# New ranks for the first and last steps of a hand-ordered two-layer kernel, and a small load on another queue

## The chip, the cores and the metric

The kernel runs on one core of a Trainium2 chip. The metric is the device time of one execution in microseconds, the median of three runs. One more execution was recorded by the hardware profiler, and all rows shown here are from it.

## The reference

Two layers, A and B, are applied twice in turn to a sequence x of 2048 rows of 640 numbers, each on the normalized sequence and with a residual:

```python
x = x + _A_ref(_layernorm(x), A_mem0, A_Wq, A_Wk, A_Wv, A_Wo, A_seg_len)
x = x + _B_ref(_layernorm(x), B_w1, B_w2, B_w3, B_w4)
x = x + _A_ref(_layernorm(x), ...)      # the same weights again
x = x + _B_ref(_layernorm(x), ...)
```

A is attention with a recurrent memory. The sequence is cut into 64 segments of 32 rows. For each segment, 8 memory rows and the 32 segment rows (40 together) go through attention with 32 heads of 192, under a causal mask that leaves the memory visible. The first 8 rows of the result are the memory of the next segment, so the segments of one layer must be done one after the other:

```python
for s in range(n_seg):
    h = concatenate([mem, x[:, s * 32:(s + 1) * 32]], axis=1)
    q, k, v = (einsum('btd,dhe->bhte', h, W) for W in (Wq, Wk, Wv))
    scores = where(mask, einsum('bhqe,bhke->bhqk', q, k) * scale, -1e9)
    o = einsum('bhte,hed->btd', einsum('bhqk,bhke->bhqe', softmax(scores), v), Wo)
    mem = o[:, :8]
    outs.append(o[:, 8:])
```

B is a mixer with an MLP: layernorm, w1 (640 x 640), GELU, four column groups shifted by one or two rows forward or back, w2 (640 x 640), a residual, layernorm, w3 (640 x 1536), GELU, w4, a residual. All data are bf16.

## The kernel before

**Lanes and steps.** The first A layer is lane 0 and the second one lane 1, five segments behind it. A step t of 69 does segment t of lane 0 and segment t - 5 of lane 1 together: 80 columns of activations per matmul where both lanes are there, which is so in steps 5 to 63. Steps 0 to 4 and 64 to 68 have one lane only (40 columns, computed 56 wide). Every second step, a chunk of 64 rows of each lane runs through B (functions `chunk` and `chunk_end`) beside the attention; chunk 0 begins in step 2, and the last chunk runs alone after step 68.

**A step.** `attention_step` goes over the 32 heads in 8 groups of 4, two groups to a pair of weight columns. For a group: keys and queries (L1638, tiles psk and psq, 30 matmuls each), the copies of them by VectorE and ScalarE, values (L1743 with one lane, tile psv, 10 matmuls of 384 columns for each half pair), scores (L1763, pss, 6 matmuls), the softmax on VectorE and ScalarE, a transpose (L1798, pst, 4), the product with the values (L1815, pso, 8), and the output projection (L1841, psy, two halves of 15). The single buffers for keys, queries and probabilities tie a group to the one before it.

**Weights.** Part of the attention weights stays in SBUF (`res_tile`, loads at L1480), the rest is streamed again in every step through a ring of 12 slots (`load_pair`, L1496); the last pair of a step is kept for the next. The weights of B go through a ring of 3 slots (`load_b`, L1532 to L1538). All of these are issued by SyncE (SP), whose list is in order: a load that waits holds those behind it. Step 0 loads all attention weights once, 31.5 MB.

**The order.** Every operation is entered with `add` in a `Plan`. Each engine has one list, sorted by the operation's `pr`, which is the start of its step (48 to a step) plus a number from the table `RANK`, found by the part's tag, the function's name and how often it came. The tags of the two-lane steps 7 to 61 are `step0` and `step1`, those of their chunks `chunk` and `chunk_end`; the steps at the two ends have tags of their own (`first`, `second`, `head2` to `head6`, `tail0` to `tail5`, `end`, `last`, `last_end`, and `chunk_0` and the like). Equal ranks are taken in the order in which they were entered:

```python
lines = {e: sorted((o for o in self.ops if o.e == e), key=lambda o: (o.pr, o.i)) for e in engines}
```

`place` then walks through the lists with a model of durations. It gives out PSUM and ring slots and says which SP loads are held back until a certain matmul is done. It never changes the order within an engine.

**The ends.** `start` loads the 8 memory rows (L2385) into `vx2`, a part of the buffer h2u that VectorE clears first, and the first 128 input rows (L2400), both on SP. At the end of a chunk, `ft4` (L2371, tile psn) transposes its normalized rows for lane 1; ScalarE copies them to where the attention reads them. In the last chunk the twelve row blocks of w4 (L2324, tile y) are taken in four parts of three, each after its GELU and for each of two column halves.

Of the kernel before, what the change touches and what calls it, by code (L numbers as in the profile page):

```python
# [8 lines left out]
ACT = mybir.ActivationFunctionType  # L9
# [64 lines left out]
        "apply_ln.f": (5823623, 14711714, 41344890, 50140480,),  # L74
        "chunk.f1": (-282353,),
        "chunk.f2": (-279353,),
        "chunk.f3": (11931231,),
        "chunk.fe": (11885669,),
        "chunk.fe3": (51644685,),
        "chunk.fel": (11888669,),  # L80
        "chunk.fhr": (29147201,),
        "chunk.fhs": (48728121,),
        "chunk.fk0": (-242386,),
        "chunk.fk1": (29099225,),
        "chunk.fs": (50134480, 50137480,),
        "chunk.ft": (276821,),
        "chunk.ftl": (16247520,),
        "chunk.fw": (27423019, 27290948, 27355567, 45544174, 42382384, 42537930, 53199095, 51647685, 52014009,
            61485311, 60294121, 61862243, 68553475,),
        "chunk.fx": (463310,),  # L90
        "chunk.fx0": (19284882, 15974063,),
        "chunk.fxu": (52262814,),
# [6 lines left out]
        "load_b.fn": (-11648251, -10043186, -10061451, 28210158, 27695754, 26335880, 37821417, 39249861,  # L99
            39863368, 52700349, 52565225, 55051271, 61800496,),  # L100
        "transposes.f": (7724019, 50355195,),
    },
    "chunk_0": {
        "apply_ln.f": (4538124, 5597588, 28417407,),
        "chunk.f1": (-57885499,),
        "chunk.f2": (-52174124,),
        "chunk.f3": (5635096,),
        "chunk.fe": (5984368,),
        "chunk.fe3": (30624721,),
        "chunk.fel": (7390477,),  # L110
        "chunk.fhr": (12978596,),
        "chunk.fhs": (21983325,),
        "chunk.fk0": (3941774,),
        "chunk.fs": (26770777, 26773777,),
        "chunk.ft": (287279,),
        "chunk.ftl": (8154259,),
        "chunk.fw": (10898172, 11428325, 9816535, 22114487, 22111506, 22106575, 35230677, 31585055, 36089115,
            42297789, 43852725, 42859895, 51136238,),
        "chunk.fx": (26689,),
        "chunk.fx0": (9696294, 8940053,),  # L120
        "chunk.fxu": (31869412,),
# [6 lines left out]
        "load_b.fn": (-50643732, -54844896, -50893189, 13355857, 10512466, 13802419, 26207666, 25044572,  # L128
            30162184, 34930868, 36974992, 36093962, 41994092,),
        "transposes.f": (5241977, 28420407,),  # L130
    },
    "chunk_1": {
        "apply_ln.f": (5188177, 5304240, 16754321, 34290954,),
        "chunk.f1": (-3885035,),
        "chunk.f2": (2878183,),
        "chunk.f3": (11030708,),
        "chunk.fe": (10677253,),
        "chunk.fe3": (35559227,),
        "chunk.fel": (14015378,),
        "chunk.fhr": (16787571,),  # L140
        "chunk.fhs": (27232205,),
        "chunk.fk0": (-2386666,),
        "chunk.fk1": (8785106,),
        "chunk.fs": (30730498, 30733498,),
        "chunk.ft": (-66578,),
        "chunk.ftl": (11033708,),
        "chunk.fw": (15374235, 15374235, 15374235, 28977346, 29252606, 27401998, 36668792, 35592102, 36728839,
            44065631, 47134963, 44719301, 50340601,),
        "chunk.fx": (480073,),
        "chunk.fx0": (12535502, 11391513,),  # L150
        "chunk.fxu": (34730386,),
# [6 lines left out]
        "load_b.fn": (-12025702, -12014120, -11721377, 20176838, 21353444, 15499060, 30530966, 28177755,  # L158
            30530966, 36977269, 38686929, 38033259, 44520182,),
        "transposes.f": (8162117, 34343668,),  # L160
    },
    "chunk_2": {
        "apply_ln.f": (4731456, 6523101, 17796726, 29088164,),
        "chunk.f1": (-17894593,),
        "chunk.f2": (2893951,),
        "chunk.f3": (6655158,),
        "chunk.fe": (7220521,),
        "chunk.fe3": (32398753,),
        "chunk.fel": (11058085,),
        "chunk.fhr": (15897759,),  # L170
        "chunk.fhs": (28856856,),
        "chunk.fk0": (2451823,),
        "chunk.fk1": (11780324,),
        "chunk.fs": (26979944, 26982944,),
        "chunk.ft": (1151586,),
        "chunk.ftl": (7727683,),
        "chunk.fw": (13670250, 13670706, 13746357, 22235702, 22955237, 26645082, 34320431, 34254360, 33960831,
            45657603, 44775551, 43775707, 61169734,),
        "chunk.fx": (273607,),
        "chunk.fx0": (10743432, 11542267,),  # L180
        "chunk.fxu": (29054564,),
# [6 lines left out]
        "load_b.fn": (-17872484, -14843409, -32827582, 17069457, 17605094, 17567464, 26421363, 26389164,  # L188
            23014726, 36743531, 42403460, 34896909, 44579461,),
        "transposes.f": (5188954, 31624248,),  # L190
    },
    "chunk_end": {
        "apply_ln.f": (92798701,),
        "chunk_end.fc": (92804701, 103908174, 95145945,),
        "chunk_end.fs": (87395771, 87477590,),
        "chunk_end.fst": (88627127, 94644354,),
        "chunk_end.ft4": (92801701,),
        "chunk_end.fw": (75064939, 84266408, 74209536, 76906110, 85870768, 84840446,),
        "chunk_loads.f": (89254710, 94354887, 91668152, 91838190, 91163514,),
        "ln_ops.f1": (88627127,),  # L200
        "ln_ops.f2": (90742589,),
        "load_b.fn": (70817954, 75700858, 60623461, 70394650, 76123229, 75884221,),
    },
    "chunk_end_0": {
        "apply_ln.f": (96080479,),
        "chunk_end.fc": (104851242, 103783179,),
        "chunk_end.fs": (86548528, 87483179,),
        "chunk_end.fst": (89850784,),
        "chunk_end.ft4": (96083479,),
        "chunk_end.fw": (62060627, 62060627, 71462733, 77227245, 76430775, 83316611,),  # L210
        "chunk_loads.f": (88185073, 89080724, 85358214,),
        "ln_ops.f1": (90380445,),
        "ln_ops.f2": (91641311,),
        "load_b.fn": (42877559, 42623100, 62941044, 70087169, 68888715, 77038207,),
    },
    "chunk_end_1": {
        "apply_ln.f": (70510275,),
# [1047 lines left out]
def kernel(  # L1265
# [1117 lines left out]
    def start():  # L2383
        def f1(op):
            nc.sync.dma_start(out=vx2[0:M, :], in_=A_mem0[0])  # L2385
# [96 lines left out]
```

## Time and profile before

| | us |
|---|---|
| median of 3 runs | 3204.87 (3199.76 to 3208.84) |
| the profiled execution | 3210.39 |
| its span, first to last instruction | 3208.7 |
| TensorE busy | 3092.8 (96%) |
| VectorE, ScalarE, GpSimd busy | 2049.6, 1712.3, 504.2 |
| TensorE busy from 300 to 600 us | 294.27 of 300 |
| TensorE busy from 0 to 300 us | 235.75 of 300 |
| TensorE busy from 2860 to the end | 318.38 of 349 |

PE is TensorE's matmul unit, PEld its weight loads, which run beside the matmuls; DVE is VectorE, ACT ScalarE, POOL GpSimd and SP SyncE. A row of the view of waits reads: who waited, at which line, for what; then the total in us, how often, and the longest. "issue" stands for idle time in which the engine waited for nothing that the profile shows. A row of the view of windows reads: from and to in us, the length, the busy us of each engine with the number of its instructions, the share of TensorE's full clock that was granted, the busy share of the DMA engines, and GB/s. A row of the timeline reads: start, length, engine, line, operation, tiles, count, and in brackets the idle time before it and what ended that. A row of the chain reads: start, length, what, count.

### The profile page before, as it was taken

To read this page: it belongs to the slowest core of one execution; us is meant where nothing else is said; L and a number is where in the kernel's file an instruction comes from. 1 tells how busy PE (TensorE), PEld (TensorE's weight loads), DVE (VectorE), ACT (ScalarE), POOL (GpSimd) and SP (SyncE) were. 2 spreads that over 40 slices of the span, in tenths; PEclk is the share of its full clock that TensorE was granted. 3 is DMA by queue.
4 is the path that set the end of the run, shared out by engine and by line. 5 is a ranking of instruction groups with operands and counts; after the bars stand their busy time and mean duration, and the time that the engine had idled before them with its cause. 6 is when DMAs were issued, how large, how long until landed. Compare 5 with 4: busy or idle time off the path is not lost.

```text
span 3208.7 us, 158772 instructions
## 1 busy us (share of the span) xinstructions
PE 3092.8 (96%) x70198; PEld 2761.7 (86%) x70201; DVE 2049.6 (64%) x6448; ACT 1712.3 (53%) x3985; POOL 504.2 (16%) x983
## 2 busy tenths in 40 slices
PE   4889999999999999999999999999999999999997
PEld 3778888888888988988889889888998888888886
DVE  2556666666666666666666666666666666666565
ACT  1334555555556555555565556555555565555443
POOL 0001111111111111111111111111111111110000
PEclk8999999999999999999999999999999999999999
DMA  9777888888888887888888888877887788888786
GB/s 362 263 258 263 262 271 258 260 264 281 260 262 283 271 259 261 266 282 259 260 284 267 256 263 267 279 258 259 282 271 256 258 279 267 261 267 282 243 291 219
DMA packets 421674, 859.45 MB, mean 268 GB/s; under 512 B 48334, under 2 KB 216223, under 8 KB 420984
## 3 DMA queue, kind: packets, MB, share of 16 engines
q1 hardware_dynamic: 396792, 796.09, 75.7%
q0 software_dynamic: 24032, 53.12, 5.2%
q8 instruction: 550, 9.01, 1.1%
q14 instruction: 140, 1.15, 0.1%
q10 hardware_dynamic: 160, 0.08, 0.0%
HBM read 823.73 MB, written 25.37 MB: 265 GB/s over the span
## 4 chain that ended last, share of the span: by engine, by line
PE 89%; DMA 5%; issue 3%; DVE 1%; ACT 1%; POOL 0%; SPq 0%; POOLq 0%; ACTq 0%; DVEq 0%
PE psq L1638 17%; PE psk L1638 17%; PE psy L1841 17%; PE psv L1685 12%; PE pso L1815 4%; PE pss L1763 4%; PE y L2317 3%; PE psh L2271 3%; PE psv L1712 3%; PE pst L1798 2%; PE psv L1743 2%; DMA V<-vahead 2%; DMA wst<-in_A_Wq_dram 2%; PE hs L2208 1%; PE psh L2148 1%
## 5 line engine op out<-in xcount | busy, mean ns | idle before, releaser
L1638 PEld LDWEIGHTS <-wst 128*128 128x128 bf16 x19872 | 830.4, 99 | 92.5 <-issue 22.3
L1841 PE MATMUL psy<-oT,wo 128*128 128x80 bf16 (+1 forms) x16560 | 679.1, 200 | 14.0 <-issue 10.0
L1673 ACT CAST V<-psv 32x384 bf16<-32x384 f32 (+3 forms) x1032 | 479.1, 473 | 376.2 <-PE psv L1685 159.8
L1841 PEld LDWEIGHTS <-wo 128*128 128x128 bf16 x16560 | 619.1, 99 | 29.0 <-issue 27.2
L1638 PE MATMUL psk<-hT,wst 128*128 128x80 bf16 (+1 forms) x9936 | 562.1, 200 | 25.6 <-DMA wst<-in_A_Wk_dram 13.0
L1638 PE MATMUL psq<-hT,wst 128*128 128x80 bf16 (+1 forms) x9936 | 540.8, 200 | 13.3 <-DMA wst<-in_A_Wq_dram 10.9
L1648 ACT CAST qT<-psq 128x480 bf16<-128x480 f32 (+1 forms) x552 | 293.8, 532 | 393.6 <-PE psq L1638 353.7
L1775 DVE CUSTOM_DVE_ANT_1 pss<-pss,mask 80x320 f32<-80x320 f32 (+2 forms) x552 | 258.8, 469 | 319.8 <-PE pss L1763 298.3
L1663 DVE CAST kT<-psk 64x160 bf16<-64x160 f32 (+1 forms) x1104 | 338.9, 307 | 84.1 <-PE psk L1638 60.5
L1823 ACT CAST oT<-pso 128x480 bf16<-128x480 f32 (+1 forms) x552 | 293.5, 532 | 161.9 <-PE pso L1815 147.2
L1782 ACT ACTIVATE Pm<-pss,sm 80x320 bf16<-80x320 f32 (+2 forms) x552 | 279.1, 506 | 165.7 <-PE pst L1798 83.1
L1786 DVE TENSOR_REDUCE sm<-Pm 80x4 f32<-80x320 bf16 (+2 forms) x552 | 251.1, 455 | 122.4 <-ACT Pm L1782 113.7
L1638 PE MATMUL psq<-hT,wq 128*128 128x80 bf16 (+1 forms) x6624 | 316.2, 200 | 8.7 <-DMA wq<-in_A_Wq_dram 5.3
L1806 ACT COPY PT<-pst 80x320 bf16<-80x320 bf16 (+2 forms) x552 | 220.7, 400 | 188.3 <-PE pso L1815 105.7
L1638 PE MATMUL psk<-hT,wk 128*128 128x80 bf16 (+1 forms) x6624 | 315.8, 200 | 2.0 <-issue 1.1
L1685 PEld LDWEIGHTS <-hT 128*128 128x128 bf16 x2320 | 206.7, 98 | 104.9 <-issue 1.0
L1656 DVE CAST kT<-psk 128x320 bf16<-128x320 f32 (+1 forms) x552 | 253.3, 459 | 55.6 <-PE psk L1638 46.5
L1638 PEld LDWEIGHTS <-wq 128*128 128x128 bf16 x6624 | 266.5, 99 | 21.9 <-issue 12.8
L1685 PE MATMUL psv<-wv,hT 128*128 128x384 bf16 x1276 | 284.1, 326 | 0.5 <-ACT V L1673 0.5
L1788 DVE TENSOR_TENSOR Pm<-Pm,sm 80x320 bf16<-80x320 bf16 (+2 forms) x552 | 255.7, 463 | 44.7 <-DVE sm L1787 1.0
L1638 PEld LDWEIGHTS <-wk 128*128 128x128 bf16 x6624 | 266.7, 99 | 3.1 <-issue 2.5
L1693 POOL DMA_DIRECT2D vahead<-V x232 | 119.5, 516 | 953.6 <-ACT V L1673 727.7
(136 smaller groups left out, 4126.4 us busy)
## 6 DMA issues: line engine op xcount, KB each, us to landing
wst<-in_A_Wk_dram SPq DMA_DIRECT2D x556, 384.0 KB, 4.7
wst<-in_A_Wq_dram SPq DMA_DIRECT2D x556, 384.0 KB, 4.8
wstB<-in_B_w_dram SPq DMA_DIRECT2D x495, 320.0 KB, 4.5
wst<-in_A_Wv_dram SPq DMA_DIRECT2D x383, 384.0 KB, 5.0
wstB<-in_B_w_dram SPq DMA_DIRECT2D x132, 160.0 KB, 4.1
vahead<-V POOLq DMA_DIRECT2D x232, 84.0 KB, 4.3
V<-vahead POOLq DMA_DIRECT2D x232, 84.0 KB, 4.7
wo<-in_A_Wo_dram SPq DMA_DIRECT2D x8, 960.0 KB, 12.3
```

What stands on the lines that cost most here:

```text
L1638: nc.tensor.matmul(out=o[:, cc, 0:W], lhsT=wv(kc, GW * j + cc * P, GW * j + (cc + 1) * P), rhs=h[:, kc, cw:cw + W], start=begin(pq), stop= ...
L1648: nc.scalar.copy(out=qT[G % QT_BUFS][:, :, c0:c0 + N], in_=T(pq)[:, :, off:off + N])
L1656: nc.vector.tensor_copy(out=k4[:, :, 0::3, c0:c0 + N], in_=p4[:, :, 0::2, off:off + N])
L1663: copy(out=k4[r0:r1, :, jj, c0:c0 + N], in_=p4[r0:r1, :, 1, off:off + N])
L1673: (nc.vector.tensor_copy if e == "DVE" else nc.scalar.copy)(out=v_part(*dst), in_=a_)
L1685: nc.tensor.matmul(out=T(bank)[:], lhsT=left[:, kc, :], rhs=wv(kc, GWH * b, GWH * (b + 1)), start=(kc == 0), stop=(kc == KC - 1))
L1775: nc.vector.tensor_tensor_reduce(out=o, in0=o, in1=maskt.unsqueeze(1).to_broadcast([NR, HG, N]), scale=-scale, scalar=3.0e38, op0=ALU.add, ...
L1782: nc.scalar.activation(out=Pb[0:NR, :, 0:N], in_=o, func=ACT.Exp, bias=sm_[0:NR, 0:1], scale=-1.0)
L1786: nc.vector.tensor_reduce(out=sm_[0:NR, 2:2 + HG], in_=Pb[0:NR, :, 0:N], axis=AX.X, op=ALU.add)
L1788: nc.vector.tensor_tensor(out=Pb[0:NR, :, 0:N], in0=Pb[0:NR, :, 0:N], in1=sm_[0:NR, 6:6 + HG].unsqueeze(2).to_broadcast([NR, HG, N]), op=A ...
L1823: nc.scalar.copy(out=o_[:, :, off:off + N], in_=T(pso)[:, :, 0:N])
L1841: nc.tensor.matmul(out=o[:, m, cw:cw + W], lhsT=wo[:, cc, m * P:(m + 1) * P], rhs=o_[:, cc, 0:W], start=st, stop=True, skip_group_check=True)
```

## The change

The table `RANK` is replaced as a whole. Its numbers are in units of 1/67108864 (2 to the 26th) where they were millionths, and `add` is changed to match. For `step0`, `step1`, `chunk` and `chunk_end` the numbers are the old ones on the new scale. For all other tags they are from a new search: the order of the one-lane steps 0 to 4 and 64 to 68, of the two-lane steps next to them, of the chunks beside these, and of the last chunk. The search's plan counted TensorE's instruction blocks; the kernel's own plan does not. Apart from that, the load of the memory rows goes to ScalarE's queue. No operation is added or left out.

```diff
     "chunk": {
-        "chunk.f3": (11931231,),
+        "chunk.f3": (800691382,),
...
     "chunk_end_tail0": {
-        "apply_ln.f": (81876355,),
-        "chunk_end.fst": (82366936, 81760822,),
-        "chunk_end.ft4": (83228689,),
-        "ln_ops.f2": (81873355,),
+        "apply_ln.f": (5872788644,),
+        "chunk_end.fst": (5628179420, 5628240926,),
+        "chunk_end.ft4": (5992579053,),
+        "ln_ops.f2": (5628142308,),
...
     "last_end": {
-        "chunk_end.fs": (27670453, 24358356,),
-        "chunk_end.fw": (21564715, 21306200, 23454463, 22051901, 27667453, 23690061, 23690061, 23690061,),
+        "chunk_end.fs": (3903370521, 3903370521,),
+        "chunk_end.fw": (3165677059, 3058847649, 3701121311, 3165878386, 3903169194, 3903169194, 3902455248,
+            3900429352,),
...
     "start": {
-        "start.f1": (-606783133,),
-        "start.f4": (-606786133,),
+        "start.f1": (-761774171496,),
+        "start.f4": (-762032755413,),
...
-        op.pr = round(1000000 * due) if k >= len(ranks) else round(1000000 * self.base) + ranks[k]
+        op.pr = round(67108864 * due) if k >= len(ranks) else round(67108864 * self.base) + ranks[k]
...
     def start():
         def f1(op):
-            nc.sync.dma_start(out=vx2[0:M, :], in_=A_mem0[0])
-        add("SP", 0.1, -90, f1, w=(B("vx2"),), dma=20000)
+            nc.scalar.dma_start(out=vx2[0:M, :], in_=A_mem0[0])
+        add("ACT", 0.1, -90, f1, w=(B("vx2"),), dma=20000)
```

Some pieces of the two orders, read from the sorted ranks:

| | before | after |
|---|---|---|
| SP's first entries | input rows, memory rows, load, load, resident tile | input rows, load, load, load, resident tile |
| last Q or K tile of step 0, MB into its loads | 26.7 | 26.0 |
| last V tile of step 0 | 27.5 | 29.5 |
| last loads of step 0 | two Wo tiles | two Wo tiles |
| matmuls between the last w4 matmul and psn, chunks tail0, tail1, tail2 | 147, 102, 72 | 282, 102, 102 |
| last w4 work of the last chunk (part of four, column half) | 3rd second half, 4th both halves, 3rd first half | 4th both halves, 3rd both halves |

More of the change, by code (lines that the diff above doesn't have):

```diff
@@ L87 @@
[L87 to L92, printed above, removed]
[6 rows of a table removed]
[L99 to L101 removed]
+        "apply_ln.f": (390816740, 987286415, 2774608591, 3364870645,),
@@ L107 @@
[L107 to L118, printed above, removed]
@@ L131 @@
+        "chunk.fx0": (367754743, 172569584,),
+        "chunk.fxu": (1938774438,),
[6 rows of a table added]
+        "load_b.fn": (-170906047654, -170906047654, -170906047654, 920004857, 882220319, 896865883,
+            1304411523, 1257239965, 1386097304, 2462708421, 2481349681, 2470811516, 2484920200,),
+        "transposes.f": (164006783, 1639917844,),
     },
     "chunk_1": {
[L133 to L136, printed above, removed]
@@ new lines @@
+        "chunk.fe": (316376284,),
+        "chunk.fe3": (1959638099,),
+        "chunk.fel": (369464748,),
+        "chunk.fhr": (778257113,),
+        "chunk.fhs": (1679713241,),
+        "chunk.fk0": (646066165,),
+        "chunk.fk1": (898552330,),
+        "chunk.fs": (1715148724, 1715350050,),
+        "chunk.ft": (57711930,),
+        "chunk.ftl": (169733834,),
+        "chunk.fw": (807022150, 806116800, 807023775, 1271841077, 1402935676, 1121619675, 2204982466,
+            1956421294, 1956443760, 2937607038, 3058004067, 2968056114, 3969956053,),
@@ L301 @@
-        "transposes.f": (6585971, 28518353,),
+        "apply_ln.f": (97288509, 505476737, 1074913445, 1893060360,),
+        "chunk.fe": (327833962,),
+        "chunk.fe3": (2026986560,),
+        "chunk.fel": (534071399,),
+        "chunk.fhr": (859836856,),
+        "chunk.fhs": (1844791763,),
+        "chunk.fk0": (266312925,),
+        "chunk.fk1": (787177492,),
+        "chunk.fs": (1674764092, 1863774978,),
+        "chunk.ft": (-23764831,),
+        "chunk.fw": (638420884, 661797947, 628306519, 1566545467, 1562896270, 1559653263, 2046135994,
+            2027187887, 2124823259, 2620748490, 2816149302, 2636649469, 3162075176,),
@@ L327 @@
-        "transposes.f": (6527484, 35837665,),
+        "apply_ln.f": (371605162, 370993904, 1393728099, 2093210348,),
+        "chunk.fe": (460332473,),
+        "chunk.fe3": (2296318838,),
+        "chunk.fel": (609297303,),
+        "chunk.fhr": (796384097,),
+        "chunk.fhs": (2296117511,),
+        "chunk.fk0": (693286516,),
+        "chunk.fk1": (693487842,),
+        "chunk.fs": (1747505621, 1942032597,),
+        "chunk.ft": (12500783,),
+        "chunk.fw": (679901984, 611651605, 752911618, 1704347815, 1714078083, 1736058533, 2660864586,
+            2596069770, 2714677185, 2972142262, 2984054357, 2984033548, 3917670881,),
@@ L351 @@
-        "load_b.fn": (-7573298, -3992147, -5434168, 18870690, 18402542, 15297474, 27659785, 24913866,
-            27115241, 35610124, 33976492, 35065580, 44270645,),
-        "transposes.f": (11703929, 31113333,),
+        "apply_ln.f": (812472994, 901319518, 1463224163, 1911689701,),
+        "chunk.fe": (875636097,),
+        "chunk.fe3": (2230136542,),
+        "chunk.fel": (875837424,),
+        "chunk.fhr": (1136613167,),
+        "chunk.fhs": (1876018868,),
+        "chunk.fk0": (574183471,),
@@ new lines @@
+        "chunk.fx": (-278567231,),
+        "chunk.fxu": (1297854132,),
+        "chunk.fz0": (-6543789675,),
+        "chunk.halves.fa": (-216070822, -216292776, 282927822, 1297416848,),
+        "chunk.halves.fn": (-216292776, -216292776,),
+        "gelu.f1": (-215890123, 248054344, 1298055458, 1304618073, 1384067416, 1320313861,),
+        "gelu.f2": (-216292776, 252139152, 1298256785, 1304416746, 1431936661, 1362814397,),
+        "gelu.f3": (252340479, 252340479, 1305020726, 1350736613, 3339755119, 1414490168,),
```

1565 lines of the change are left out of this document (803 added, 762 removed), and 300 rows, old and new, of the table RANK.

## The prediction

> **What bounds the kernel now.** I read the page's summary first, then the busy shares by slice, then the chain.
>
> ```profile
> span 3208.7 us, 158772 instructions
> PE 3092.8 (96%) x70198; PEld 2761.7 (86%) x70201; DVE 2049.6 (64%) x6448; ACT 1712.3 (53%) x3985; POOL 504.2 (16%) x983
> PE   4889999999999999999999999999999999999997
> q8 instruction: 550, 9.01, 1.1%
> PE 89%; DMA 5%; issue 3%; DVE 1%; ACT 1%; POOL 0%; SPq 0%; POOLq 0%; ACTq 0%; DVEq 0%
> ```
>
> TensorE is busy 96% of the span and carries 89% of the chain. It is short of nine tenths only in the first three slices and the last, and those, with the one-lane steps in them, are all that this change reorders. I therefore sorted the ranks of the diff (they are the sort keys of each engine's list, so the diff gives the order outright). For the 55 two-lane steps 7 to 61 and their chunks the new ranks are the old ones times 67.108864, the ratio of the two scales, and the order is the same on SP, ACT, DVE and (one instruction at the edge apart) POOL. On TensorE the two halves of one output projection, 15 matmuls each on the same operands, swap in the even steps: nothing. So every gain or loss must come from the first 300 us and the last 290 us.
>
> The fourth row is the key to those parts. 550 packets of 9.01 MB make 16.4 KB each, and TensorE's 70198 matmuls and 70201 weight loads over 550 give 255 instructions a packet: TensorE's code arrives in blocks of about 128 matmul pairs. The next view counts matmuls (the x behind PE busy) between starts that the trace marks as idle "issue", that is, waiting for nothing it can see.
>
> ```profile
> 106.60:125.61 19.01, 17.68 (x512) 14.90 (x511) 11.01 (x44) 8.42 (x26) 0.00 (x0) 1.00 0.90 307
> ...
> 165.54:186.65 21.11, 17.73 (x510) 15.39 (x511) 11.79 (x45) 8.48 (x26) 0.00 (x0) 0.99 0.75 238
> 186.65:209.94 23.29, 21.30 (x512) 17.52 (x511) 11.25 (x43) 8.45 (x25) 0.79 (x2) 0.93 0.92 309
> 209.94:236.00 26.06, 22.47 (x639) 19.44 (x639) 17.99 (x68) 9.98 (x32) 4.73 (x9) 0.93 0.66 222
> ```
>
> 512, 510, 512 and 639 are four, four, four and five times 128. The unexplained stalls sit on the block boundaries. What they cost in the one-lane steps, at the head (95 to 262 us) and then at the tail (2960 to 3181 us):
>
> ```profile
> PE psy L1841 <- issue: 5.1, 5, 1.5
> PE pso L1815 <- issue: 3.2, 2, 1.8
> PE psq L1638 <- issue: 2.2, 2, 1.8
> ...
> PE psk L1638 <- issue: 0.4, 1, 0.4
> ```
>
> ```profile
> PE psn L2371 <- DVE h2u L1911: 2.4, 2, 1.8
> PE psy L1841 <- issue: 1.7, 3, 1.2
> PE psq L1638 <- DMA wst<-in_A_Wq_dram: 1.6, 2, 1.4
> PE psv L1743 <- issue: 1.4, 2, 0.9
> ...
> PE psh L2271 <- issue: 1.0, 1, 1.0
> PE pst L1798 <- issue: 1.0, 1, 1.0
> ```
>
> Head: 5.1 + 3.2 + 2.2 + 0.4 = 10.9 us. Tail: 1.7 + 1.4 + 1.0 + 1.0 = 5.1 us. Together 16.0 us, and no other wait in these parts comes near that.
>
> The first step is another matter:
>
> ```profile
> 5.00:10.00 5.00, 1.93 (x27) 1.56 (x28) 1.01 (x4) 0.58 (x3) 2.98 (x6) 1.00 0.86 285
> 10.00:50.00 40.00, 12.35 (x282) 11.48 (x279) 4.15 (x19) 1.93 (x6) 0.00 (x0) 0.79 1.03 393
> 50.00:87.50 37.50, 28.09 (x549) 20.67 (x547) 13.62 (x50) 9.98 (x30) 1.16 (x3) 0.77 1.05 381
> 87.50:94.30 6.80, 4.55 (x105) 4.06 (x106) 2.43 (x11) 2.05 (x6) 0.49 (x1) 0.75 0.63 173
> ```
>
> The last two columns are the share of the DMA engines and GB/s. From about 6 to 87.5 us they are full at 381 to 393 GB/s. The four attention weights are 4 x 640 x 6144 x 2 bytes = 31.5 MB, 81 us at that rate. So step 0 is bound by the transfers until 87.5 us, and then TensorE works another 6.8 us.
>
> **A. Memory rows by ScalarE's queue.**
>
> ```profile
> SPq L2385 <- DVE h2u L1416: 2.9, 1, 2.9
> 0.82 0.41 SPq L2400 DMA_DIRECT2D vbg<-in_A_x_dram  x1
> ...
> 4.10 0.36 SPq L2385 DMA_DIRECT2D h2u<-in_A_mem_dram  x1
> 4.50 0.83 SPq L1496 DMA_DIRECT2D wst<-in_A_Wk_dram  x2
> ```
>
> SP issues the input rows at 0.82 us, then waits 2.9 us for VectorE's clearing of the buffer that takes the memory rows, and every weight load of step 0 is queued behind that wait. In the new order the second entry of SP's list is a weight load into a free slot, so the stream can start at 1.2 us instead of 4.5: 2.9 + 0.36 = 3.3 us, in a stage where the transfers set the end. On ScalarE the moved load waits for the same clearing; behind it there stand only the copies of those rows, which need it anyway, and ScalarE has nothing else before 6 us. If the stream were not bound by its start, only the issue (0.36) would be saved. I take 3.3. [...]
>
> **B. The order of step 0.** Both orders end their loads with the last two Wo tiles (0.98 MB each). In the old one TensorE is behind its data: the last Q, K tile is the 26.7th MB and the last V tile the 27.5th, some 10 us before the end of the stream, yet 105 matmuls and the last softmax groups remain after it. The new one brings the last Q, K tile at 26.0 MB, has all eight score blocks issued before the last V tile (29.5 MB, 5 us before the end), and after the last two Wo tiles only four projections of 15 matmuls are left. Those cost
>
> ```profile
> 71.41 1.73 PE psy L1841 x60
> ```
>
> so at best 6.8 - 1.9 = 4.9 us go; at worst V comes 2 MB later (5 us) and nothing is gained, or a block of code lands late, as it did once in this step, and 2 us are lost. I take 2.0.
>
> **C. Fewer short blocks.** Of the mix that fills blocks,
>
> ```profile
> 102.59 0.93 PE psk L1638 x36
> ...
> 109.29 0.92 PE psv L1743 x10
> ```
>
> a narrow matmul takes 26 ns and a value matmul 92 ns. A block of 128 narrow ones is 3.3 us of work, one with 20 value matmuls 4.65 us. Between boundaries that stall, the four-block stretch of 19.01 us shows 4.75 us a block. I counted the work of each block in both orders from such rows and summed what each lacks to 4.3 us, the figure that gives 10.8 us for the old head, close to the 10.9 measured. The new order gives 8.3 at the head (where the value matmuls had come 40 in one block and none in the next, they are now 20 and 20), and 13.4 against 15.8 at the tail. Scaled to the measured stalls: 10.9 x 2.5/10.8 = 2.5 us and 5.1 x 2.4/15.8 = 0.8 us. Sum 3.3; bounds: 3 worse, since a shift of a few instructions moves every boundary, and 8 better, half of all. The tail is overcounted by this method, which is why I scale it.
>
> **D. The clock behind the stalls.** The granted clock is 1.00 in most stretches, but 0.93 in the two that follow the stalls of 1.8 and 1.5 us, and
>
> ```profile
> 2960.00:2980.00 20.00, 18.21 (x396) 15.24 (x394) 10.87 (x32) 11.68 (x27) 3.86 (x7) 0.91 0.54 176
> ```
>
> 0.91 here, where the 1.8 us wait of psn lies. That is 0.07 x 23.29 + 0.07 x 26.06 + 0.09 x 20 = 5.2 us of TensorE's clock. It comes back only where the long stall goes: between 0 and 5.2, I take half, 2.6. [...]
>
> **E. Waits for the normalized chunk.** psn transposes what VectorE normalizes. Between the last w4 matmul and psn the old order has 147 matmuls in the first tail chunk, the new 282; 135 more at 26 ns are 3.5 us against the 1.8 us wait. In the third tail chunk 72 become 102: 0.8 us against 0.6. GpSimd's power step also comes ahead of the output store there. Gain 2.4, at worst 0: the rows that psn feeds are due at the next step's start, 4 us of matmuls later.
>
> **F. The very end.**
>
> ```profile
> 3202.46 1.80 PE L2324 MATMUL y<-wst,h2u 128*128 128x320 bf16 x12 [0.52 <-DVE h2u L1952]
> ```
>
> Twelve matmuls follow the last GELU. In the new order the six on the part that VectorE finishes earlier go first: 0.9 us off the path, or 0. The rest of the last chunk, with the same VectorE list but for the two final sums, stays.
>
> Sum: 3.3 + 2.0 + 3.3 + 2.6 + 2.4 + 0.9 = 14.5 us. The profiled execution took 3210.39 us (span 3208.7 and 1.7 around it), so 3195.9 for it; the median of the runs is 3204.87, 5.5 lower, and the same 14.5 off it gives **3190.4 us**.
>
> **Rivals.** *1. The order gives nothing back, only the queue and the end do.* Fetches are shifted, other blocks are short, another wait follows where psn's was. Then A and F remain, 4.2 us: 3200.7, within 0.3%, which is about what a measurement of this kernel can tell from no change. For it: the shortfall drops by under a quarter, and the sum has six terms of guesses. Against it: A and E each rest on a row of their own.
>
> *2. Slower: a weight load moved ahead blocks SP's list.* SP issues in order and its ring has 12 slots. Step 0's loads move by up to 31 places, those of steps 1 to 4 by up to 8. A load put ahead of its free slot holds all behind it. The 1.6 us row of psq shows what that costs: up to 1.4 us of TensorE for a load, and a clock dip (1.7) if two fall together, so about 4.5 us for a step with two such loads. With three such steps of the nine one-lane ones the gain is gone; with six it is 27 - 14.5 = 12.5 us slower, 3217. The point from which it decides is over five steps. Against it: in the new order of step 0 each ring load has its slot released by matmuls whose data lie at least 5.1 MB ahead in the stream (3.5 in the old), and the DMA engines are at 0.66 to 0.92 in the one-lane stretches above, not full.
>
> *3. The change does nothing.* If the wait of SP merely moves and the plan's slots undo the order: 3205. Hardly: the orders do differ.
>
> **How the numbers follow.** Forecast 0.62, rival 1 0.24, rival 2 0.11, rival 3 0.03. A gain of more than 0.3% (9.6 us) is the forecast's case: 0.62; within 0.3% are rivals 1 and 3: 0.27; slower 0.11. The good ends sum to 3.3 + 4.9 + 8 + 5.2 + 2.4 + 0.9 = 24.7, 3180, and the bad ends of the orders leave rival 1's 3200.7; with the runs' spread of 4 us either way (3199.76 to 3208.84) the range reaches from 3178 to 3208.
>
> **What would show it.** The first weight load on SP at about 1.3 us and no wait for h2u there; the DMA engines full until about 84 and step 0's last projection by 90; "issue" before TensorE about 8.4 us at the head and 4.3 at the tail; psn without a wait and 1.00 at that place; half as many matmuls after the last GELU. It is wrong if TensorE's waits for wst grow in steps 1 to 4 or 64 to 68, if new clock dips appear, or if the stretch from 300 to 2860 us, which must stay as long as it was, changes by more than 2 us.

## The result, and the profile after

| | before | after |
|---|---|---|
| median, us (12 runs each) | 3206.43 (3199.71 to 3214.18) | 3194.65 (3184.41 to 3202.14) |
| ratio of the runs | | 0.9962, 95% interval 0.9948 to 0.9977 |
| profiled execution, us | 3210.39 | 3194.27 |

The changed kernel is faster by 11.8 us, where 14.5 were forecast (3190.4). A second comparison later, five runs against 29, gave 0.9949 (0.9934 to 0.9965). The page after, with the rows that answer to those of before:

```profile
span 3192.6 us, 158772 instructions
PE 3085.9 (97%) x70199; PEld 2758.7 (86%) x70201; DVE 2050.3 (64%) x6448; ACT 1710.0 (54%) x3985; POOL 502.2 (16%) x983
PE   4899999999999999999999999999999999999998
```

The engines have the same work, TensorE is busy 7 us less and the span is 16.1 us shorter. Where the time came from is read by cutting both spans at the same events: the ends of step 0, 4, 62, 63 and 67 (VectorE's copy of the new memory rows, L1873 and L1868, now L1942 and L1937). The view of windows over these six stages, first before, then after (length, busy us with instruction counts, then granted clock, DMA share, GB/s at the end):

```profile
0.00:94.26 94.26, 46.91 (x954) 37.76 (x955) 24.99 (x94) 15.82 (x46) 8.98 (x33) 0.80 0.95 347
94.26:258.46 164.20, 147.30 (x4025) 125.59 (x4025) 100.19 (x381) 64.56 (x195) 8.59 (x17) 0.97 0.79 261
258.46:2931.96 2673.50, 2650.65 (x58926) 2389.13 (x58923) 1755.50 (x5389) 1512.89 (x3421) 467.77 (x896) 1.00 0.82 267
2931.96:2983.73 51.77, 48.68 (x1143) 42.52 (x1143) 26.94 (x82) 28.17 (x62) 3.86 (x7) 0.97 0.67 221
2983.73:3144.46 160.73, 149.66 (x4054) 128.30 (x4054) 107.58 (x393) 69.48 (x200) 13.41 (x26) 1.00 0.85 281
3144.46:3208.69 64.23, 49.62 (x1099) 38.39 (x1101) 34.38 (x116) 21.36 (x61) 1.56 (x4) 0.99 0.67 220
```

```profile
0.00:89.97 89.97, 46.67 (x954) 38.03 (x955) 25.07 (x94) 15.30 (x45) 8.96 (x33) 0.89 0.99 364
89.97:245.80 155.83, 140.97 (x4025) 122.15 (x4025) 101.21 (x381) 64.81 (x196) 8.30 (x17) 1.00 0.83 276
245.80:2921.54 2675.74, 2651.14 (x58923) 2388.92 (x58921) 1754.96 (x5389) 1510.88 (x3420) 466.45 (x896) 1.00 0.82 266
2921.54:2968.48 46.94, 46.70 (x1148) 40.85 (x1146) 26.60 (x81) 28.88 (x64) 3.80 (x7) 1.00 0.75 249
2968.48:3127.88 159.40, 148.77 (x4054) 128.80 (x4054) 108.47 (x392) 69.20 (x199) 13.24 (x27) 1.00 0.84 284
3127.88:3192.58 64.70, 51.61 (x1100) 39.95 (x1101) 34.02 (x116) 20.90 (x61) 1.47 (x3) 0.97 0.66 218
```

By this one pair: step 0 -4.3, steps 1 to 4 -8.4, the middle +2.2, step 63 -4.8, steps 64 to 67 -1.3, the end +0.5. It misleads. In steps 1 to 4 the granted clock rose from 0.97 to 1.00 and TensorE's busy time for the same 4025 matmuls fell by 6.3 us, and whether that belongs to the new order or to this execution a pair of profiles can't say. Kernels that carry the old order in one stage and the new in another give several profiles of each order. They come from several sessions and chips, which this table does not keep apart. Lengths of the stages, in us, means with lowest and highest:

| stage | old order | new order | difference |
|---|---|---|---|
| step 0 | 93.9 (5 profiles, 92.6 to 94.3) | 90.2 (5, 89.6 to 90.7) | -3.7 |
| steps 1 to 4 | 160.1 (6, 157.2 to 164.2) | 155.3 (5, 153.4 to 158.5) | -4.9 |
| steps 5 to 62, the same order from 7 to 61; old or new head | 2673.9 (6, 2671.6 to 2675.8) | 2673.8 (5, 2668.4 to 2677.8) | 0 |
| step 63 | 50.2 (5, 48.9 to 51.8) | 46.8 (6, 46.8 to 46.9) | -3.4 |
| steps 64 to 67 | 162.4 (6, 160.3 to 167.4) | 161.3 (5, 159.4 to 162.7) | -1.1 |
| after step 67 | 66.1 (7, 64.2 to 68.1) | 64.8 (4, 63.6 to 66.2) | -1.3 |
| sum | | | -14.4 |

The two comparisons of whole runs, 0.38% and 0.51%, are 12 and 16 us; the sum of the stages lies between them. Steps 5, 6 and 62 have new orders too: by the same ends of steps, step 6 takes 44.9 us with the new head and 45.6 with the old one (means), and steps 5 and 62 are alike within 0.1. (The kernels with doubled transposes and with the thin stream, below, are left out of the table, but for step 0 of the latter, whose order and load are the old ones.)

### The profile page after: what moved, and what is told of

Read it like the earlier page. It is cut to its first block, busy times and chain, and to the rows that moved or that the text cites. A ratio compares the mean times of both kernels' runs of the same rounds, so it can differ in the third digit from the quotient of the medians.

```text
span 3192.6 us, 158772 instructions
## 1 busy us (share of the span) xinstructions
PE 3085.9 (97%) x70199; PEld 2758.7 (86%) x70201; DVE 2050.3 (64%) x6448; ACT 1710.0 (54%) x3985; POOL 502.2 (16%) x983
## 5 line engine op out<-in xcount | busy, mean ns | idle before, releaser
L1742 ACT CAST V<-psv 32x384 bf16<-32x384 f32 (+2 forms) x1032 | 478.4, 472 | 380.4 <-PE psv L1754 160.9
```

What stands on the lines that cost most here:

```text
L1742: (nc.vector.tensor_copy if e == "DVE" else nc.scalar.copy)(out=v_part(*dst), in_=a_)
```

## The experiments

In the kernels with a part of the new order the table is on the new scale, and the numbers of the tags that are not named are the old ones times 67.108864. All medians are set against runs of the kernel before on the same chip in the same session: 3209.60 (27 runs) for the first four, 3207.19 (29) for the next four, 3209.31 (11) for the last four.

**1. The queue alone.**

```diff
-            nc.sync.dma_start(out=vx2[0:M, :], in_=A_mem0[0])
-        add("SP", 0.1, -90, f1, w=(B("vx2"),), dma=20000)
+            nc.scalar.dma_start(out=vx2[0:M, :], in_=A_mem0[0])
+        add("ACT", 0.1, -90, f1, w=(B("vx2"),), dma=20000)
```

> The kernel before with its old order, and only the load of the memory rows on ScalarE's queue. Theory 1 (step A of the prediction): the weight stream starts at about 1.3 us instead of 4.5 and everything up to the end of step 0 moves up by it; the DMA engines are full until about 84.2 us instead of 87.5, step 0 ends 3.3 us earlier (at 91.0 instead of 94.26), and the run is 3.3 us shorter (3203, ratio 0.9990). [...] Theory 3 (the stream moves, but the later stages wander by more than that): step 0 ends 3.3 us earlier, and the whole run is not shorter.

Measured: 3207.09, ratio 0.9989 (0.9976 to 1.0002). Step 0 ends at 90.92. The timeline of SP:

```profile
0.82 0.40 SPq L2400 DMA_DIRECT2D vbg<-in_A_x_dram  x1
1.29 0.88 SPq L1496 DMA_DIRECT2D wst<-in_A_Wk_dram  x2
2.21 0.43 SPq L1480 DMA_DIRECT2D wk<-in_A_Wk_dram  x1
```

The weights start 3.2 us earlier than the 4.50 of before, and step 0 ends 3.0 us under the old mean of 93.9. Theory 1 holds for the stage; the issue alone is 0.36 us by the row of before. The run's gain of 3.5 us by the ratio has zero just inside its interval.

**2. The order of step 0 alone, with the queue.** Tags `start` and `first`:

```diff
     "start": {
...
-        "start.f4": (-606786133,),
+        "start.f4": (-762032755413,),
```

> Step 0 alone in its new order (the tags start and first), memory rows by ScalarE's queue, all other orders as before. Theory 1 (A and B of the prediction, with the measured end of step 0 in the changed kernel): step 0 ends at about 90, 4.3 us earlier than before, of which 3.3 are the queue and 1.0 the order; the steps 1 to 4 then take 164 us as before, or less by up to 2 us only, since their order is the old one; run 4 us shorter (3202, 0.9987). Theory 2 (the order of steps 1 to 4 is not what gained 8.4 us there; their clock dips were a matter of phase): steps 1 to 4 take some 156 to 160 us here already, and TensorE's busy time for their 4025 matmuls falls from 147.3 to about 141; run 8 to 12 us shorter.

Measured: 3205.28, ratio 0.9990 (0.9974 to 1.0005). Step 0 ends at 89.58, steps 1 to 4 take 162.4 us. Theory 1 by the length. But TensorE's busy time there is 142.93 us at a clock of 1.00, nearer to the 141 of theory 2 than to 147.3: the half clock of the first profile is not the order's, and neither theory had both.

**3. The head, 4. the tail.** All tags from `start` to `head6` with chunks 0 to 2, and all from `tail0` to `last_end`, the latter with the load on SP:

```diff
     "second": {
...
-        "attention_step.values.fv": (213518, 1901075, 16800798, 16413487, 23499711, 26489622, 39468084,
-            40772489,),
+        "attention_step.values.fv": (12649327, 12649343, 902609968, 903262489, 1557299857, 1553934805, 2337335395, 2736195414,),
```

```diff
     "chunk_end_tail0": {
...
-        "chunk_end.ft4": (83228689,),
+        "chunk_end.ft4": (5992579053,),
```

> All orders of the head (start to head6 and chunks 0 to 2) new, those of the tail old, memory rows by ScalarE's queue. Theory 1 (each part of the change gains where it stands): steps 0 to 4 end at 245.8 as in the changed kernel (258.5 before), the tail from step 63 to the end takes 276.8 us as before (271.0 in the changed kernel), so the run is 9 to 12 us shorter (3195 to 3198, 0.9965), less what the unchanged middle gives back (up to 3.9 us in the profiled runs). Theory 2 (the middle gives back by rule what the head gained, since its blocks and loads fall otherwise): the stretch of steps 5 to 62 takes 2676 us and more, and the run is only 6 us shorter.

> All orders of the tail (tail0 to end, last and their chunks) new, head as before, memory rows on SP as before. Theory 1 (E and C of the prediction in the tail; profiled: step 63 by 4.8 us, steps 64 to 67 by 1.3, the last chunk 0.5 longer): from the end of step 62 to the end of the run 271 us instead of 276.8; no wait before psn; run 5.6 us shorter (3201, 0.9983). Theory 2 (the tail's gain in the profiled run was the clock dip alone, which comes and goes between runs): 2.4 to 3 us shorter. Theory 3 (the order of the tail gains nothing): within 1 us of before.

Measured: head 3197.24, 0.9962 (0.9944 to 0.9979); tail 3198.91, 0.9967 (0.9953 to 0.9981). Both parts are worth something by themselves. Together they would make 23 us, more than the change ever gave, and more than their stages hold: head -8.6, tail -5.8 in the table above. In its profile the tail kernel is 3.1 us shorter than the old mean after step 62, and its middle, in the old order, 2.3 us shorter than the mean. Why its runs were some 5 us better than that was not found.

**5. The changed kernel again, 6. the kernel before again.** No edit.

> The changed kernel once more, unaltered. Theory 1 (the gains of the parts stand, and what differs from execution to execution is chance): the end of step 0 at 90 and step 63 in 47 us as before, steps 1 to 4 between 156 and 159 us, the 28 short (even) two-lane steps of the middle scattered again by 0 to 3 us above 39.27, other steps than last time; run 3190 to 3200, 10 to 14 us under the kernel before. Theory 2 (the middle is longer by rule, 2675.7 us, in the changed kernel): the middle within 1 us of 2675.7, and the same steps long as in the first profile (20, 36 and 38). If head and tail add up as their separate runs gave (12.2 and 10.6 us under the kernel before), the run is 23 us shorter; if those two runs were 5 us too favourable each, 12.

> The kernel before once more, unaltered. Theory 1 (its first profile was unlucky in steps 1 to 4: the same order took 164.2 us there and 160.6, 162.4 and 158.3 us in three kernels that keep it): steps 1 to 4 take about 160.5 us, TensorE's busy time there 143 and not 147.3, clock 0.99 to 1.00; step 0 ends at 94.1 as before; step 63 takes 49.5 to 51.8 with its 1.8 us wait before psn, since that wait hangs on VectorE's list and not on luck; middle between 2669 and 2678. Theory 2 (the half clock in steps 3 and 4 belongs to the old order): 164 us and clock 0.97 again.

Measured: after 3191.59, 0.9949 (0.9934 to 0.9965); before 3209.46, 1.0005 (0.9994 to 1.0017). Before, steps 1 to 4 took 158.15 us now and TensorE was busy 143.20 of them at 1.00, 6 us less than in the first profile of the same kernel. After took 154.74 there, so the second pair differs by 3.4 us where the first differed by 8.4. After, the middle was 2673.81 and not 2675.74, and steps 20, 36 and 38 were not the long ones again. Theory 1 came nearer both times, with misses: steps 1 to 4 of after lie under its 156 to 159, and step 0 of before ended at 92.60 where it had 94.1. Steps 1 to 4 of before again (old order), of the kernel of experiment 3 and of after again (both new order):

```profile
92.60:250.75 158.15, 143.20 (x4025) 122.56 (x4025) 100.05 (x381) 64.52 (x195) 8.57 (x17) 1.00 0.82 272
```

```profile
90.49:249.01 158.52, 144.06 (x4025) 123.60 (x4025) 101.64 (x382) 64.95 (x196) 8.30 (x17) 0.98 0.81 271
```

```profile
90.36:245.10 154.74, 140.79 (x4025) 121.97 (x4025) 101.36 (x381) 64.81 (x196) 8.31 (x17) 1.00 0.83 278
```

**7. Step 63 alone.** Tags `tail0`, `tail1`, `chunk_tail0`, `chunk_end_tail0`, so the edit of experiment 4 for these four.

> The new order for the steps 62 and 63 and the chunk beside them alone (tags tail0, tail1, chunk_tail0, chunk_end_tail0); head, later tail and the queue as before. Theory 1 (E of the prediction, with the half clock that follows the wait): no wait before psn in step 63, which takes 46.8 us instead of 50.5 (mean of four profiles with the old order), clock 1.00; the steps 64 to 67 as in the old order (160.7 to 167.4); run 3.7 us shorter (0.9988). Theory 2 (only the wait of 1.8 us goes, the clock falls elsewhere): 48.7 us. Theory 3 (the rows that psn feeds come too late for the next step and the wait moves to the matmuls of step 64): step 63 shorter, step 64 (39.0 us) longer by as much.

Measured: 3207.94, 1.0004 (0.9992 to 1.0015). Step 63 of four kernels: before again and experiment 2 in the old order, then after again and this kernel in the new one:

```profile
2925.00:2973.93 48.93, 46.80 (x1143) 40.87 (x1143) 26.93 (x81) 27.97 (x62) 3.85 (x7) 1.00 0.71 233
```

```profile
2927.67:2978.09 50.42, 48.30 (x1143) 42.41 (x1143) 26.92 (x82) 28.02 (x62) 3.85 (x7) 0.97 0.68 227
```

```profile
2918.91:2965.68 46.77, 46.53 (x1149) 40.82 (x1146) 26.62 (x82) 28.89 (x64) 3.79 (x7) 1.00 0.75 248
```

```profile
2927.26:2974.03 46.77, 46.54 (x1148) 40.84 (x1146) 26.61 (x81) 28.70 (x63) 3.80 (x7) 1.00 0.76 250
```

46.77 twice: the wait before psn is gone, step 64 is not longer (38.5 us), so the stage is as theory 1 said. The first two rows show the same 1.8 us wait before psn; once the clock fell after it and once not, and that is 1.5 us. The run did not get shorter: 3.7 us expected, and the interval reaches to 2.6. The middle of its profile is 2675.76, 1.9 over the mean, and that is all that the profile offers: why the run did not gain is open.

**8. 60 more matmuls ahead of everything.**

```diff
-            for m in range(KC):
+            for m in [k % KC for k in range(13 * KC - 1)] + [KC - 1]:
                 nc.tensor.transpose(out=T(p0)[:, m, :], in_=vx2[0:M, m * P:(m + 1) * P], identity=ident[0:M, 0:M])
```

> The kernel before with the five transposes of the memory rows, in its first 5 us, done 13 times over (60 matmuls more, the same results written again), nothing else altered: every later matmul stands 60 places further in TensorE's code. Theory 1 (C of the prediction: the unexplained stalls belong to the boundaries of blocks of 128 matmuls): the stalls of the one-lane steps keep their places in the count of matmuls (number modulo 128 between 86 and 93 at the head), so they meet other operations than before, 60 matmuls earlier in the order; the head's stalls sum to about the same 10 us with another pattern, the tail's to 5 to 6. Theory 2 (the stalls belong to operations that wait for something which the profile does not show): the same operations stall (psy, pso and psq in the same groups), and the number modulo 128 is 60 further (18 to 25). In both the 60 transposes themselves cost under 2 us, in a stage that the transfers bound: run within 0.2% of before.

Measured: 3210.07, 1.0011 (0.9999 to 1.0024). Stalls of over 0.2 us at the head, at five places that both kernels share, with the number that the stalled matmul has in the count of all matmuls:

| number (modulo 128) | before again | before with 60 more |
|---|---|---|
| 1499 (91) | psy, 0.8 us | psy, 1.4 us |
| 1755 (91) | psy, 1.2 | psq, 2.7 |
| 2775 (87) | psy, 1.2 | psq, 1.1 |
| 4308 (84) | psy, 0.8 | psk, 1.0 |
| 4436 (84) | psq, 1.3 | psq, 0.8 |

The three other stalls of the shifted kernel's head, at 2520, 3797 and 4819, have 88, 85 and 83. The windows between the starts of the table in the shifted kernel count 2, 8 and 12 blocks:

```profile
111.50:123.25 11.75, 8.95 (x256) 7.48 (x255) 4.59 (x19) 3.00 (x9) 0.00 (x0) 1.00 0.91 299
123.25:164.79 41.54, 37.69 (x1020) 31.75 (x1020) 27.36 (x103) 16.95 (x51) 2.29 (x5) 0.96 0.69 230
164.79:223.24 58.45, 54.52 (x1533) 47.04 (x1533) 37.95 (x143) 24.95 (x76) 5.29 (x9) 1.00 0.85 286
```

The operations moved by 60 and the stalls did not: they belong to the places in the code. (The count slips by one now and then, where the trace lacks a record.) In the profiles of before and after, the nine stalls of over 1 us in steps 1 to 4 each ended 1.28 to 1.59 us after one of the 550 packets of the row `q8 instruction` (16.4 KB, one to some 128 matmuls) had landed.

**9. The load back on SP, 10. the old last chunk, 11. the changed kernel with 60 more matmuls.** Experiment 1 reversed in the changed kernel, the old numbers for `last` and `last_end`, and the edit of experiment 8.

```diff
-            nc.scalar.dma_start(out=vx2[0:M, :], in_=A_mem0[0])
+            nc.sync.dma_start(out=vx2[0:M, :], in_=A_mem0[0])
...
     "last_end": {
-        "chunk_end.fs": (3903370521, 3903370521,),
+        "chunk_end.fs": (1856932667, 1634661600,),
...
```

> The changed kernel with the load of the memory rows back on SP, all orders new. Theory 1 (A of the prediction, from the other side): SP waits again for the clearing of h2u by VectorE, some 2.9 us, ahead of the weight stream, and step 0 ends at 93 instead of 90.0 to 90.5; all later stages as in the changed kernel (steps 1 to 4 in 154.7 to 158.5 us, step 63 in 46.8); run 3 us longer than the changed kernel, 0.9960 to 0.9965 of the kernel before. Theory 2 (only the issue): step 0 ends at 90.5.

> The changed kernel with the old order of the last chunk (tags last and last_end). Theory 1 (F of the prediction was worth nothing, because a wait for ScalarE's GELU before the w3 matmuls, 1.5 us, came in where the waits before psv and y went): from the end of step 67 to the end of the run 64.2 to 66.7 us as in the kernels with the old order, against 64.7 to 66.2 with the new: within 1 us. Theory 2 (F as predicted): 0.9 us longer than with the new order, 65.6 to 67, with psv waiting 1.7 us for VectorE and twelve matmuls after the last GELU.

> The changed kernel with the five transposes of the memory rows done 13 times over (60 matmuls more, the same results again), so that every block boundary falls 60 matmuls earlier in the new order. Theory 1 (C of the prediction: the new order is fitted to where the boundaries fall): the stalls keep their numbers in the count of matmuls and meet other operations; by the count of what each block lacks to 4.3 us the head goes from 8.3 to 9.0 and the tail from 9.2 to 13.1, so the measured sums go from 8.4 (mean of three) to 9 at the head and from 5.3 to 7.5 at the tail; run 3 us longer than the changed kernel. Theory 2 (the new order has more even blocks wherever they begin, or the difference in stalls is chance): 8.4 and 5.3 within their scatter of 1.5, run as the changed kernel.

Measured: 3195.73, 0.9954 (0.9941 to 0.9967); 3193.57, 0.9952 (0.9938 to 0.9967); 3197.04, 0.9959 (0.9947 to 0.9970). The three differ by less than their intervals tell apart, so the stages decide.

With the load on SP step 0 ends at 92.38, 2.2 us later than with the new order and ScalarE's queue. SP's timeline (this kernel's lines have other numbers) gives a reason why not 3: in the new order one weight load goes ahead of the wait.

```profile
0.82 0.41 SPq L2017 DMA_DIRECT2D vbg<-in_A_x_dram  x1
1.29 0.41 SPq L1113 DMA_DIRECT2D wst<-in_A_Wk_dram  x1
4.11 0.35 SPq L2002 DMA_DIRECT2D h2u<-in_A_mem_dram  x1
4.50 0.35 SPq L1113 DMA_DIRECT2D wst<-in_A_Wq_dram  x1
```

With the old last chunk the part after step 67 takes 68.1 us, longer than either theory gave; of the two, theory 2 comes nearer. VectorE's final sums, before, after, and in the changed kernel with the old last chunk, with the time that it waited for the last y:

```profile
3203.90 0.90 DVE L2332 SCALAR_TENSOR_TENSOR vbg<-y,xw 128x320 bf16<-128x320 f32 x2 [1.49 <-PE y L2324]
```

```profile
3187.83 0.90 DVE L2401 SCALAR_TENSOR_TENSOR vbg<-y,xw 128x320 bf16<-128x320 f32 x2 [0.81 <-PE y L2393]
```

```profile
3189.43 0.90 DVE L1949 SCALAR_TENSOR_TENSOR vbg<-y,xw 128x320 bf16<-128x320 f32 x2 [1.49 <-PE y L1941]
```

With 60 more matmuls the stalls at the head sum to 3.5 us (9.0 expected by counting what blocks lack), those at the tail to 8.1 (7.5 expected). Steps 1 to 4 take 151.4 us, the least of all. In this one profile the new head lost nothing by having its boundaries moved, and the count missed the sum of its stalls. At the tail the count came near, but that shows little: the kernel of experiment 9, whose boundaries are not moved, has 7.4 us there.

**12. A thinner stream.** In the kernel before:

```diff
+        shared = kind == "q" and due > 1.5 * STEP
         for j, kc in enumerate(range(nres, KC)):
+            if shared:
...
+                    nc.sync.dma_start(out=thin[:, 8 * i:8 * i + 8], in_=w_src[kind][:, kc, 0:8])
...
+                slots.append(last_k[0][j])
+                continue
```

> The kernel before with part of its stream left out: from step 1 on the query weights that come through the ring are not loaded (each such load moves 2 KB into a small tile of its own instead of 393 KB), and the queries take the slots with the key weights, so the output is another one. TensorE's instructions and all orders are the old ones; the DMA share in the one-lane steps falls from 0.82 to about 0.55. It asks why a block of code lands late. Theory 1 (only the block counts: less work in a block than its fetch takes): the unexplained stalls stay, 9 to 11.5 us at the head, and the even steps of the middle keep their mean of 39.9 to 40.1 us against a shortest of 39.27. Theory 2 (the fetch queues behind the weights on the DMA engines): the head's stalls fall to under 4 us, the even steps to 39.3 to 39.5, the run by 20 us and more.

Measured: 3185.33, 0.9924 (0.9910 to 0.9938). Steps 1 to 4 and the middle, to be read beside the rows of before above:

```profile
94.34:249.59 155.25, 144.09 (x4025) 123.90 (x4025) 100.00 (x381) 64.52 (x195) 8.57 (x17) 0.99 0.65 201
249.59:2912.75 2663.16, 2645.03 (x58926) 2387.41 (x58923) 1755.57 (x5390) 1509.01 (x3421) 466.50 (x896) 1.00 0.65 200
```

At a DMA share of 0.65 (0.55 was expected) the head's stalls fall from a mean of 10.1 us to 5.2, and the even steps 12 to 60 from means of 39.85 to 40.06 us to 39.63. With the same TensorE code in the same order that is half of theory 2 at the head; that the fetch queues behind the weights is not shown by it. This is one profile; in steps 63 to 67 the stalls were 5.7 us, no less than with the full stream (5.0 to 6.5, and 10.4 once); and the kernel of experiment 9, with the full stream, has a mean of 39.68 in the even steps. Waits for the query weights went with the loads, so not all of the 24 us comes from the stalls.

## Why the prediction came out, step by step

**A, 3.3 us: right.** 3.0 in the kernel with the queue alone, 2.2 taken back in the other direction. ScalarE was not idle before 6 us, as the prediction had it: it loads a table for 1.28 us, at 2.71 us before and, behind the moved load, at 4.73 us after. Step 0 ended earlier all the same. The DMA engines were full until 84.2, as forecast (windows of after; the last column but one is the DMA share):

```profile
50.00:84.20 34.20, 25.52 (x510) 19.12 (x509) 11.38 (x40) 8.19 (x25) 0.00 (x0) 0.77 1.05 376
84.20:91.00 6.80, 4.93 (x134) 4.12 (x131) 2.67 (x9) 2.42 (x7) 1.65 (x3) 1.00 0.57 183
```

**B, 2.0: 0.7.** From the queue alone (90.92) to the new order (mean 90.2). The work after the last load did not fall from 6.8 us to the least possible 1.9 (89.97 - 84.2 = 5.8).

**C, 3.3: 1.9 measured at the head, nothing sure at the tail, its reason not borne out.** The stalls of over 0.2 us sum to 10.1 (six profiles, old) and 8.2 (five, new) in steps 1 to 4, and to 6.5 (six) and 5.9 (five) in steps 63 to 67: 1.9 and 0.6 less. The 0.6 hangs on one profile with 10.4 (experiment 1); without it the old order has 5.7, so at the tail nothing is shown. In the profile of after the head's are

```profile
PE psy L1910 <- issue: 2.8, 3, 2.3
PE psq L1707 <- issue: 2.7, 4, 1.3
PE pss L1832 <- issue: 2.2, 1, 2.2
PE psk L1707 <- issue: 1.5, 2, 1.4
```

9.2 us, where 8.4 were forecast. That stalls sit on block boundaries is shown by experiment 8 (numbers of 83 to 91 modulo 128 at the head of both kernels). That the new order loses less because its blocks are fitted to them is not: experiment 11 moved the boundaries, and the head lost still less. Why it loses less stays open. What one block loses varied between 0.5 and 2.0 us at the same matmul of the same order (the 3285th, six profiles), so sums of single profiles scatter by 2 us and more.

**D, 2.6: the step that failed, at the head.** It took the half clock of one execution for a property of the order. Before again had none at 186 and 210 us; the kernel with the new head and the old tail had two in steps 1 to 4. Over all profiles TensorE's mean busy time in steps 1 to 4 is 143.8 us old and 141.3 new, but the profiles without a dip differ by nearly as much (142.8 to 143.2 against 140.4 to 141.0, 2.3 in the mean). So nearly all of these 2.5 us is not the clock, and the sum had no term for it. Of the 2.3 us, 1.6 are fewer gaps of 0.13 to 0.2 us between the starts of two matmuls, which the page counts as busy (in after, 29.3 us of such gaps leave 0.01 us idle): 196 to 199 of them in steps 1 to 4 in the four profiles of the old order without a dip, 186 to 190 in the four of the new one. Most of the rest goes with longer gaps, of which the new order has some six fewer: the page counts about 0.2 us of each as busy. Why the new order has fewer of them was not found. The size of D's head part came out by luck. Its tail part, half of 0.09 x 20 or 0.9 us, was as forecast: the wait of psn went, and with it a half clock that cost 1.5 us in three of the five old profiles, 0.9 in the mean.

**E, 2.4: right.** The wait before psn is gone in all six profiles with the new order of step 63, where it had been 1.8 us in every old one. So is the one of 0.6 us in step 67, in the five profiles with the new order there. Step 63 gained 3.4 in all: besides the 1.8, the 0.9 of the clock, a wait of 0.3 us for hT at the start of the step, and a stall in the first profile.

**F, 0.9: 0.7 at the place it named.** VectorE waits 0.81 us instead of 1.49 between the last GELU's product and the final sum, the same in every profile of each order. The stage gained 1.3, with a scatter of 4 us; in the first pair it had seemed 0.5 longer.

**The rivals.** The first (only A and F) falls with step 63 and steps 1 to 4. The second did not come: waits for weights in steps 1 to 4 were 0 and 0.4 us in the two profiles of before and 0.8 and 3.1 in those of after, but 3.3 also in the old order of experiment 2. By two of its own signs the prediction would have been wrong: new clock dips appeared (two in steps 1 to 4 of the kernel with the new head), and the middle of the first pair grew by 2.2 us. Both came with the old order too. The bound that the middle must hold within 2 us was too tight: with one and the same order from step 7 to 61 it scatters from 2668 to 2678.

So the sum of 14.5 against 14.4 by the stages is partly luck: B was too large by 1.3, C by 1.4, and the 1.7 of D's head part was replaced by another cause, of 2.5. The parts that have a row or a count of their own make 3.0 + 0.7 + 1.9 + 2.5 + 3.4 + 0.6 + 0.7 = 12.8 us (A, B, the stalls and the busy time of steps 1 to 4, step 63, psn in step 67, F); the 1.6 left are within the scatter of the stages. Where the gain lies is shown; why steps 1 to 4 gained their 4.9 us is not.

## What to carry to other kernels

Cut both spans at the same events and compare stages, but take several executions before a stage's difference is believed: here one pair showed 8.4 us in a stage where the means give 4.9, and a gain of 0.7 us that every profile has at its place looked like a loss of 0.5. A wait in front of the first transfer of a stage that the transfers bound can be worth its full length: here 2.9 us of waiting and 0.36 of issuing gave 3.0. A price read off one execution's clock should enter a sum with its chance, not as a property of the order.

## What the runs showed of the hardware

The middle, with one and the same order in steps 7 to 61, accounts for a part of the spread of the runs. There nearly every odd step from 11 to 61, cut at the ends of steps, takes 52.02 us, in every execution alike. An even one takes 39.27 us at the least and 39.7 to 40.1 in the mean, with up to 3.1 us more in single steps, mostly other steps each time (36 and 60 are long more often than the rest). Over the 25 even steps from 12 to 60 that adds up to 10 to 21 us in 13 profiles. The view of waits lists only part of it, mostly as "issue" (1.4 to 9.4 us in these steps).

In the one-lane steps and step 63 the clock was halved for 3.4 us at a time after stalls of 1.4 to 2.7 us, but not after all of them: the 1.8 us wait before psn was followed by it in four profiles of seven, and stalls of 2.2 and 2.3 us in after were not. In the 14 profiles 15 such dips began in steps 1 to 67. In 14 of the 15, TensorE idled for 1.5 to 2.3 us of the 3.4 just before the dip, and for 1.3 in the other; but stretches of 3.4 us at the same phase with up to 1.8 us idle had none after them. In the first profile of before all changes of the clock lie whole multiples of 3.413 us apart. Its three dips in these steps, at 186.43, 210.32 and 2971.70 us, are 3.413 us long each at a clock of 0.50, and TensorE had idled for 1.72, 1.60 and 1.79 us of the 3.413 before them; the stretch of the same phase from 234.2 us has 1.80 us idle, and no dip follows. What decides whether one follows was not found.

With a thinner weight stream, at a DMA share of 0.65 instead of some 0.82, the stalls of steps 1 to 4 that the profile gives as "issue" were 5.2 us, against 9.1 to 11.5 in six profiles. Those of steps 63 to 67 did not fall (5.7 us, against 5.0 to 6.5, and 10.4 once).
